# Row loads, an output slot and operand sums moved at the seam between two stages of a fused attention and gMLP kernel

## The chip, the cores and the metric

The kernel runs on one core of a Trainium2 chip. Its time is the device time of one execution in microseconds (us); eight runs of the kernel before gave a median of 776.43, from 775.05 to 778.31. The core has a matrix engine (TensorE, PE in the profile), a vector engine (VectorE, DVE), an activation engine (ScalarE, ACT), a general engine (GpSimd, POOL) and an engine that here only issues transfers (SyncE, SP). Each engine works through its own list of instructions in order and waits on semaphores for the others.

## The reference

The kernel computes a residual attention block and a residual gated MLP over 2048 tokens of width 1024. The part around the change is the MLP's gating, `_B_ref`:

```python
z = gelu(einsum('bsd,df->bsf', x, w_in))
z1 = z[..., :Fh]                       # Fh = 1792
z2 = layernorm(z[..., Fh:])
g = einsum('ts,bsf->btf', w_sp, z2) + b_sp[None, :, None]
return einsum('bsf,fd->bsd', z1 * g, w_out)
```

`w_sp` is 2048 x 2048 and `b_sp` has one value for each output token t.

## The kernel before

The kernel is one straight program. Every operation is recorded in program order, a recorder works out from the memory cells that each one reads and writes which others it has to wait for, and then each engine's list is emitted. There is no planner at run time: the order of the Python calls is the order of each engine's queue, transfers included (those of `sp` stand in SP's queue, those of `act` in ACT's).

The stages are attention with its output projection, then `z2` (the second half of the MLP's input, normalized and kept in fp16), then `z1` (the first half), then gating with the spatial matrix in two passes of 1024 output tokens each (`pr` 0 and 1), each followed by the product with `w_out`.

Both z1 and gating replace eight block products of a 2 x 2 block matrix product by seven, in a Strassen-like scheme, so both need sums of operands.

**z1.** `z1_step(g, k)` for 14 groups g and seven products k each (four matmuls per product). The steps run in the order of 7g + `offs[k]`; the last five are (13, 2) at 95 after (13, 7) at 94, then (12, 3) at 96, (13, 4) at 97 and (13, 3) at 103. Steps 6, 7, 4 and 3 are followed by adds on DVE into one of the `ZT` tiles, and `z1_out` on ACT writes the gelu into `Z1T`. The sums of weight blocks (`sz_sum`) run on POOL. With `on(g, k, f, ...)` other work is hung behind a step: the transposing loads of the four blocks of `w_sp` (`sp_load`, on SP's queue, at steps (6, 3), (8, 3) and (10, 3)), and their scaling to fp16 (`sp_part`, on ACT, groups 8 to 12).

**Operands of gating.** `b11`, `b12`, `b22` and `b21` are the scaled blocks of `w_sp`, 128 x 4096 each. `sp_sum` forms `t1 = b12 - b11`, `t2 = b22 - t1`, `t3 = b22 - b12` (into the memory of `b12`) and `t4 = b21 - t2`, for the first pass in four pieces of 128 x 1024, with a chosen engine for each piece. `s_sum(k, g)` forms the four sums `SS[:, 0]` to `SS[:, 3]` of blocks of `z2` for group g, 128 x 1024 each, on DVE; the second reads the first and the fourth reads the second.

**A group of gating.** `gate_group(pr, g, ba, bd, nx)` for g from 0 to 6. A product (`prod`) is eight matmuls into one of eight PSUM banks. `ba` holds the first product, `Z2 x b11`, made one group earlier. ACT copies it, scaled, to `s1`. POOL adds a row of biases to it twice, giving `s1b2` and `s1b1`. DVE then reads the other products with `stt` (bank times a scale plus an operand) and multiplies the four results into `Z1T` with `out`. The tiles `s1`, `s1b1`, `s1b2`, `u2` and `u3` exist once, so a group's values wait for the readers of the group before. In the first pass, groups 0 and 1 get both their first products (`b11` and `b21`) before group 0 starts: `pre` makes four products right after z1.

**Bias rows.** `brow_load(pr)` loads two stretches of 512 values of `b_sp`, each repeated on all 128 partitions, into `BROW[0]` and `BROW[1]` (at 205 K and 206 K of each partition's memory), with two transfers on SP's queue. The fifth slot of the weight sums `SZ` (used by z1 for odd groups) lies at 206 K too. After the row loads the same queue issues the two loads of `w_out` (`WO0`).

The seam between the stages in program order is: last z1 step; `t1` and `t2` in four pieces each; `s_sum` 1 to 4 for group 0; `brow_load(0)`; the `WO0` loads; four products; `gate_group(0, 0)`.

Of the kernel before, what the change touches and what calls it, by code (L numbers as in the profile page):

```python
# [6 lines left out]
F16 = mybir.dt.float16  # L7
# [251 lines left out]
def bass_sequential_preLN__memory_aug_infini_attn__mixer_gmlp__prompt_kernel(  # L259
# [17 lines left out]
    pe, act, dve, pool, sp = R.pe, R.act, R.dve, R.pool, R.sp  # L277

    K = 1024
# [4 lines left out]
    def tens(name, shape, dt, off):  # L284
        sz = int(np.prod(shape[1:])) * mybir.dt.size(dt)
        assert off % 32 == 0 and off + sz <= ARENA, (name, off, sz)
        t = nc.alloc_sbuf_tensor_at(name, list(shape), dt, offset=abase + off)
        R.space[t[:].tensor.name] = ("sbuf", off)
        return t

    class Bump:
# [4 lines left out]
        def __call__(self, name, shape, dt):  # L296
# [73 lines left out]
          for k, o in ROLES + (("t1", 126), ("t2", 190), ("t3", 22), ("t4", 38))}  # L370
# [3 lines left out]
           4: Z1X[:, 8:12, 1536:2048]},  # L374
          {1: tens("ht1", [128, 4, L], F16, 190 * K), 2: tens("ht2", [128, 4, L], F16, 194 * K),
           3: tens("ht3", [128, 4, L], F16, 38 * K), 4: tens("ht4", [128, 4, L], F16, 198 * K)}]
    SZ = [tens("sz%d" % i, [128, 4, 128], F16, o * K) for i, o in enumerate((58, 59, 60, 61, 206))]
    ZT = [tens("zt%d" % i, [128, L], F32, o * K) for i, o in enumerate((4, 6, 8, 10, 202, 12))]
    b3 = Bump(dead, 4 * K)
    ZST = b3("zst", [128, NTC, 4, 6], F32)  # L380
# [15 lines left out]
    BROW = [tens("brow%d" % i, [128, L], BF16, (205 + i) * K) for i in range(2)]  # L396
# [7 lines left out]
    def bank(b):  # L404
        return PS[:, b, :]
# [7 lines left out]
    def next_bank():  # L413
        b = rot["banks"][rot["n"] % len(rot["banks"])]
        rot["n"] += 1
        return b
# [555 lines left out]
    def sz(g, k):  # L972
        return SZ[k - 1 + (k == 4 and g % 2)][:]

# [75 lines left out]
    def sp_sum(o, r=None, eng=dve):  # L1050
        a, b = SUMS[o]
        s = slice(0, 8) if r is None else slice(2 * r, 2 * r + 2)
        eng.tensor_tensor(BH[o][:, s, :], BH[a][:, s, :], BH[b][:, s, :], ALU.subtract)

    def a_blk(i, j, g):
        f = 896 * i + 128 * g
        return Z2H[:, 8 * j:8 * j + 8, f:f + 128]

    def s_sum(k, g):
        if k == 1:  # L1060
            dve.tensor_tensor(SS[:, 0], a_blk(1, 0, g), a_blk(1, 1, g), ALU.add)
        elif k == 2:
            dve.tensor_tensor(SS[:, 1], SS[:, 0], a_blk(0, 0, g), ALU.subtract)
        elif k == 3:
            dve.tensor_tensor(SS[:, 2], a_blk(0, 0, g), a_blk(1, 0, g), ALU.subtract)
        else:
            dve.tensor_tensor(SS[:, 3], a_blk(0, 1, g), SS[:, 1], ALU.subtract)

    def prod(b, a, w, first):
        for i in range(8):  # L1070
            pe.matmul(bank(b), a[:, i, :], BH[w][:, i, :], start=(first and i == 0), stop=(i == 7),
                      skip_group_check=True)

    def prod1(g):
        b = next_bank()
        prod(b, a_blk(0, 0, g), "b11", True)
        return b
# [6 lines left out]
    def gate_group(pr, g, ba, bd=None, nx=True):  # L1084
        t1, t2 = slice(1024 * pr, 1024 * pr + 512), slice(1024 * pr + 512, 1024 * pr + 1024)
        s1, s1b1, s1b2, u2, u3 = (TMP[k][:] for k in ("s1", "s1b1", "s1b2", "u2", "u3"))
        inv = INV[0][:]

        def stt(o, b, add):
            dve.scalar_tensor_tensor(o, bank(b), inv, add, ALU.mult, ALU.add)  # L1090

        def out(v, i, t):
            z = Z1T[:, g + 7 * i, t]
            dve.tensor_tensor(z, v, z, ALU.mult)

        act.activation(s1, bank(ba), ACTF.Copy, scale=inv)
        pool.tensor_tensor(s1b2, s1, BROW[1][:], ALU.add)
        pool.tensor_tensor(s1b1, s1, BROW[0][:], ALU.add)
        if pr == 0 and g == 0:
            for r in range(4):  # L1100
                sp_sum("t3", r, pool if r < 2 else dve)
        bb, bc = next_bank(), next_bank()
        prod(bb, SS[:, 1], "t2", True)
        prod(bc, SS[:, 0], "t1", True)
        stt(u2, bb, s1b2)
        if pr == 0 and g == 0:
            for r in range(4):
                sp_sum("t4", r, pool if r < 2 else dve)
        nb = prod1(g + 1) if bd is None and g < 6 and nx else None
        if g < 6:  # L1110
            s_sum(1, g + 1)
            s_sum(2, g + 1)
        prod(bb, SS[:, 2], "t3", False)
        if bd is None:
            prod(ba, a_blk(0, 1, g), "b21", False)
        elif nx:
            nb = prod1(g + 2)
        stt(u3, bb, s1b2)
        stt(u3, bc, u3)
        out(u3, 1, t2)  # L1120
        if g < 6:
            s_sum(3, g + 1)
        prod(bb, a_blk(1, 1, g), "t4", False)
        stt(s1, ba if bd is None else bd, BROW[0][:] if bd is None else s1b1)
        out(s1, 0, t1)
        prod(bc, SS[:, 3], "b22", False)
        stt(s1b1, bb, s1b1)
        out(s1b1, 1, t1)
        stt(u2, bc, u2)
        out(u2, 0, t2)  # L1130
        if g < 6:
            s_sum(4, g + 1)
        return nb
# [17 lines left out]
    def brow_load(pr):  # L1151
        for k in range(2):
            t = 1024 * pr + 512 * k
            sp.dma_start(BROW[k][:], B_b_sp[t:t + 512].partition_broadcast(128))
# [8 lines left out]
    def z1_step(g, k):  # L1163
        p, fc = divmod(g, 7)
        s1, u2, u3 = ZT[g % 2][:], ZT[2 + g % 3][:], ZT[5][:]
        ka = {1: wz_blk(0, 0, fc), 2: wz_blk(0, 1, fc), 3: sz(g, 4), 4: wz_blk(1, 1, fc), 5: sz(g, 1),
              6: sz(g, 2), 7: sz(g, 3)}[k]
        kb = {1: hb(0, 0, p), 2: hb(1, 0, p), 3: hb(1, 1, p), 4: HT[p][4], 5: HT[p][1], 6: HT[p][2], 7: HT[p][3]}[k]
        first = k in (1, 6, 5)
        r = {1: 0, 2: 0, 6: 1, 7: 1, 4: 1, 5: 2, 3: 2}[k]  # L1170
        if first:
            zb[g, r] = next_bank()
        b = bank(zb[g, r])
        for i in range(4):
            pe.matmul(b, ka[:, i, :], kb[:, i, :], start=(first and i == 0), stop=(i == 3), skip_group_check=True)
        if k == 1:
            act.activation(s1, b, ACTF.Copy)
        if k == 6:
            dve.tensor_tensor(u2, b, s1, ALU.add)
        if k == 5 and g < 13:  # L1180
            for x in (1, 2):
                sz_sum(g + 1, x)
        if k == 7:
            dve.tensor_tensor(u3, b, s1, ALU.add)
            dve.tensor_tensor(u3, bank(zb[g, 2]), u3, ALU.add)
            z1_out(fc + 7, 2 * p + 1, u3)
            if g < 13:
                sz_sum(g + 1, 3)
        if k == 2:
            z1_out(fc, 2 * p, b)  # L1190
            if g == 0:
                sz_sum(1, 4)
        if k == 4:
            dve.tensor_tensor(s1, b, s1, ALU.add)
            z1_out(fc + 7, 2 * p, s1)
        if k == 3:
            dve.tensor_tensor(u2, b, u2, ALU.add)
            z1_out(fc, 2 * p + 1, u2)
            if g < 12:
                sz_sum(g + 2, 4)  # L1200
        for f, a in todo1.get((g, k), ()):
            f(*a)

    def on(g, k, f, *a):
        todo1.setdefault((g, k), []).append((f, a))
# [10 lines left out]
    for n, (k, g) in enumerate((("b11", 8), ("b12", 9), ("b22", 10), ("b21", 12))):  # L1216
        for r in range(4):
            on(g, (6, 7, 2, 4)[r], sp_part, k, r)
    offs = {1: -5, 6: 0, 5: 1, 7: 3, 2: 4, 4: 6, 3: 12}
    for x, g, k in sorted((7 * g + offs[k], g, k) for g in range(14) for k in offs):  # L1220
        z1_step(g, k)
    for k in ("t1", "t2"):
        for r in range(4):
            sp_sum(k, r)
    for k in range(1, 5):
        s_sum(k, 0)
    brow_load(0)
    for i in range(2):
        sp.dma_start(WO0[i][:], wout[:, 7 * i:7 * i + 7, 0:512])

    units = [(tc, 0, 512) for tc in range(6)] + [(tc, 512, 512) for tc in range(8)] + [(tc, 0, 512) for tc in (6, 7)]
    pre = [(prod1(g), prod2(g)) for g in range(2)]
    nb2 = gate_group(0, 0, *pre[0])
    nb = gate_group(0, 1, *pre[1])
    gate_group(0, 2, nb2, nx=False)
    for g in range(3, 7):
        nb = gate_group(0, g, nb)
# [73 lines left out]
```

## Time and profile before

| | |
|---|---|
| median of eight runs | 776.43 us (775.05 to 778.31) |
| profiled execution | 776.08 us, span of its instructions 774.3 us |
| busy PE / DVE / ACT / POOL | 753.2 / 552.0 / 373.7 / 293.1 us |
| z1's last matmuls, then the four products of `pre` | until 491.8, then 491.78 to 498.85 us |
| first pass of gating (first `t2` product to last `b22` product) | 504.50 to 589.5 us |
| second pass of gating | 637.65 to 723.5 us |

All times in the traces are microseconds from the start of the span, of one profiled execution. A line of a timeline gives the start, the duration, the engine, the operation with output and inputs by the program's names, the shape, and how many instructions are merged; in brackets stands the idle time of the engine before it and what ended that. `zt` are the z1 adds' tiles, `t1h` to `t4h` the fp16 sums of `w_sp` blocks, `ss` the sums of `z2` blocks, `tmp_s`, `tmp_s1b` and `tmp_u` are `s1`, (`s1b1`, `s1b2`) and (`u2`, `u3`). The chain of waits is followed back from the last instruction: each piece of it is work that the end waited for. Every operation is recorded through one helper, so all have the same line number and are told apart by tile.

### The profile page before, as it was taken

To read this page: it belongs to the slowest core of one execution; us is meant where nothing else is said; L and a number is where in the kernel's file an instruction comes from. 1 tells how busy PE (TensorE), PEld (TensorE's weight loads), DVE (VectorE), ACT (ScalarE), POOL (GpSimd) and SP (SyncE) were. 2 spreads that over 40 slices of the span, in tenths; PEclk is the share of its full clock that TensorE was granted. 3 is DMA by queue.
4 is the path that set the end of the run, shared out by engine and by line. 5 is a ranking of instruction groups with operands and counts; after the bars stand their busy time and mean duration, and the time that the engine had idled before them with its cause. 6 is when DMAs were issued, how large, how long until landed. Compare 5 with 4: busy or idle time off the path is not lost.

```text
span 774.3 us, 13304 instructions
## 1 busy us (share of the span) xinstructions
PE 753.2 (97%) x5422; PEld 361.2 (47%) x5496; DVE 552.0 (71%) x956; ACT 373.7 (48%) x433; POOL 293.1 (38%) x430
## 2 busy tenths in 40 slices
PE   8999999999999999999999999789999999999998
PEld 3445555455555545455554444334444444444444
DVE  5586589768964676659867975899895566889422
ACT  6777876787777677156966799500000000000000
POOL 2564556555553333100089887441330002223000
PEclk9999999999999999999999999989999999999999
DMA  9554555353425332797510074300038950000122
GB/s 300 169 153 89 97 83 124 82 97 84 97 55 130 90 82 42 198 248 226 182 58 1 1 133 92 102 1 1 0 55 145 242 191 8 1 0 1 62 82 75
DMA packets 138078, 75.08 MB, mean 97 GB/s; under 512 B 98336, under 2 KB 128800, under 8 KB 138016
## 3 DMA queue, kind: packets, MB, share of 16 engines
q1 hardware_dynamic: 130768, 67.40, 36.0%
q10 hardware_dynamic: 7248, 6.82, 3.0%
q8 instruction: 43, 0.70, 0.4%
q14 instruction: 19, 0.16, 0.1%
HBM read 42.74 MB, written 8.39 MB: 66 GB/s over the span
## 4 chain that ended last, share of the span: by engine, by line
PE 77%; DVE 11%; ACT 4%; DMA 3%; issue 3%; POOL 2%; ACTq 0%; POOLq 0%; DVEq 0%
PE ps L210 77%; ACT sj L210 3%; DVE ss L210 2%; DMA sj<-in_B_w_sp_dram 2%; DVE tmp_u L210 2%; DVE z1T L210 1%; ACT z L210 1%; POOL sz L210 1%; POOL zrs L210 1%; DMA wv<-in_A_wv_dram 1%; DVE stats L210 1%; DVE zt L210 1%; DVE t2h L210 1%; DVE tmp_s L210 0%; DVE tmp_s1b L210 0%
## 5 line engine op out<-in xcount | busy, mean ns | idle before, releaser
L210 ACT ACTIVATE e<-ps 128x2048 bf16<-128x2048 f32 (+1 forms) x96 | 152.6, 1590 | 41.7 <-PE ps L210 41.4
L210 POOL TENSOR_SCALAR_AFFINE_SELECT e<-e 128x512 bf16<-128x512 bf16 x128 | 90.8, 722 | 132.0 <-ACT e L210 131.9
L210 ACT ACTIVATE tmp_s<-ps,inv 128x512 f32<-128x512 f32 x14 | 9.6, 688 | 208.8 <-DVE z1T L210 146.9
L210 POOL TENSOR_TENSOR tmp_s1b<-tmp_s,brow 128x512 f32<-128x512 f32 x28 | 43.0, 1555 | 175.9 <-ACT tmp_s L210 165.9
L210 PE MATMUL ps<-win,hnT 128*128 128x448 bf16 x512 | 98.4, 352 | 0.0
L210 PE MATMUL ps<-w_out,z1T 128*128 128x512 bf16 x328 | 73.2, 379 | 0.4
L210 PEld LDWEIGHTS ps<-win,hnT 128*128 128x128 bf16 x512 | 49.6, 98 | 46.3 <-issue 0.2
L210 DVE TENSOR_TENSOR fin<-fin,ps 128x512 bf16<-128x512 bf16 (+2 forms) x33 | 21.9, 670 | 56.8 <-PE ps L210 41.0
L210 DVE TENSOR_TENSOR zt<-ps,zt 128x512 f32<-128x512 f32 x70 | 47.7, 688 | 20.6 <-PE ps L210 17.2
L210 PE MATMUL ps<-xnT,wk 128*128 128x512 bf16 x233 | 59.6, 380 | 1.2
L210 PE MATMUL ps<-wv,xnT 128*128 128x512 bf16 x255 | 59.5, 380 | 1.2 <-DMA wv<-in_A_wv_dram 0.8
L210 PE MATMUL ps<-wo,oT 128*128 128x512 bf16 x254 | 57.7, 380 | 0.1
L210 PE MATMUL ps<-xnT,wq 128*128 128x512 bf16 x226 | 54.0, 379 | 1.6
L210 PEld LDWEIGHTS ps<-w_out,z1T 128*128 128x128 bf16 x336 | 32.9, 98 | 39.7
L210 ACT ACTIVATE z<-ps 128x448 bf16<-128x448 f32 x60 | 30.6, 550 | 34.9 <-PE ps L210 34.9
L210 PEld LDWEIGHTS ps<-v,e 128*128 128x128 bf16 x1280 | 38.8, 96 | 14.0 <-issue 6.5
L210 DVE BATCH_NORM_STATS2 zst<-z 128x6 f32<-128x448 bf16 x64 | 37.8, 608 | 8.6 <-ACT z L210 8.5
L210 PE MATMUL ps<-v,e 128*128 128x33 bf16 x1280 | 42.2, 178 | 0.0
L210 DVE RECIPROCAL rd<-ps 128x16 f32<-128x16 f32 x32 | 8.0, 250 | 47.0 <-PE ps L210 46.8
L210 PEld LDWEIGHTS ps<-wo,oT 128*128 128x128 bf16 x256 | 24.1, 98 | 27.5
L210 PEld LDWEIGHTS ps<-xnT,wk 128*128 128x128 bf16 x256 | 22.6, 98 | 29.9 <-issue 5.0
L210 PEld LDWEIGHTS ps<-wv,xnT 128*128 128x128 bf16 x256 | 23.1, 98 | 28.1 <-DMA wv<-in_A_wv_dram 1.5
(168 smaller groups left out, 1381.0 us busy)
## 6 DMA issues: line engine op xcount, KB each, us to landing
sj<-in_B_w_sp_dram SPq DMA_DIRECT2D x16, 512.0 KB, 3.5
xch<-in_A_x_dram SPq DMA_DIRECT2D x16, 256.0 KB, 3.6
xr<-in_A_x_dram SPq DMA_DIRECT2D x16, 256.0 KB, 4.1
out_dram<-hch SPq DMA_DIRECT2D x16, 256.0 KB, 2.4
win<-in_B_w_in_dram SPq DMA_DIRECT2D x4, 896.0 KB, 5.3
wz<-in_B_w_in_dram SPq DMA_DIRECT2D x6, 512.0 KB, 7.4
wo<-in_A_wo_dram SPq DMA_DIRECT2D x1, 2048.0 KB, 8.4
fin<-out_dram ACTq DMA_DIRECT2D x16, 128.0 KB, 3.4
```

The costliest lines, as they stand in the source:

```text
L210: ins = getattr(e, op.name)(*op.args, **op.kw)
```

## The change

Five edits are made. The fifth `SZ` slot moves from 206 K to 204 K. `brow_load(0)` is issued behind z1 step (7, 3) instead of after z1. The four pieces of `t1` are formed behind z1 step (12, 3), so ahead of steps (13, 4) and (13, 3). `s_sum` 3 and 4 of group 0 move from the end of z1 into group 0, ahead of the `t3` and ahead of the `t4` pieces; and of the `t3` pieces POOL forms one (the first) instead of two, DVE three. In every group of both passes the first output is formed in `u3` instead of `s1`.

```diff
-    SZ = [... for i, o in enumerate((58, 59, 60, 61, 206))]
+    SZ = [... for i, o in enumerate((58, 59, 60, 61, 204))]
...
         pool.tensor_tensor(s1b1, s1, BROW[0][:], ALU.add)
         if pr == 0 and g == 0:
+            s_sum(3, 0)
             for r in range(4):
-                sp_sum("t3", r, pool if r < 2 else dve)
+                sp_sum("t3", r, dve if r else pool)
         bb, bc = next_bank(), next_bank()
         prod(bb, SS[:, 1], "t2", True)
         prod(bc, SS[:, 0], "t1", True)
         stt(u2, bb, s1b2)
         if pr == 0 and g == 0:
+            s_sum(4, 0)
             for r in range(4):
                 sp_sum("t4", r, pool if r < 2 else dve)
...
-        stt(s1, ba if bd is None else bd, BROW[0][:] if bd is None else s1b1)
-        out(s1, 0, t1)
+        stt(u3, ba if bd is None else bd, BROW[0][:] if bd is None else s1b1)
+        out(u3, 0, t1)
...
+    for r in range(4):
+        on(12, 3, sp_sum, "t1", r)
+    on(7, 3, brow_load, 0)
+
     offs = {1: -5, 6: 0, 5: 1, 7: 3, 2: 4, 4: 6, 3: 12}
     for x, g, k in sorted((7 * g + offs[k], g, k) for g in range(14) for k in offs):
         z1_step(g, k)
-    for k in ("t1", "t2"):
-        for r in range(4):
-            sp_sum(k, r)
-    for k in range(1, 5):
-        s_sum(k, 0)
-    brow_load(0)
+    for r in range(4):
+        sp_sum("t2", r)
+    s_sum(1, 0)
+    s_sum(2, 0)
```

More of the change, by code (lines that the diff above doesn't have):

```diff
@@ L376, in bass_sequential_preLN__memory_aug_infini_attn__mixer_gmlp__prompt_kernel @@
            3: tens("ht3", [128, 4, L], F16, 38 * K), 4: tens("ht4", [128, 4, L], F16, 198 * K)}]
-    SZ = [tens("sz%d" % i, [128, 4, 128], F16, o * K) for i, o in enumerate((58, 59, 60, 61, 206))]
+    SZ = [tens("sz%d" % i, [128, 4, 128], F16, o * K) for i, o in enumerate((58, 59, 60, 61, 204))]
     ZT = [tens("zt%d" % i, [128, L], F32, o * K) for i, o in enumerate((4, 6, 8, 10, 202, 12))]
```

## The prediction

> **What bounds the kernel now.** The page's first part has TensorE (PE) busy 97% of the span, so a change can pay only where PE stands still. The page's row of slices dips to 7 and 8 in one place alone, 484 to 523 us, where the clock's row dips too: the seam where z1 ends and gating begins. Next I read the chain that ended last there:
>
> ```profile
> 491.98 0.69 DVE zt L210
> 492.67 2.40 DVE t1h L210 x4
> 495.07 4.33 DVE t2h L210 x4
> 499.40 2.53 DVE ss L210
> ...
> 501.96 6.20 DVE ss L210 x3
> ...
> 509.42 1.28 DVE t3h L210 x2
> ```
>
> From the last z1 add at 491.98 to the first read of group 0's second product (`stt(u2, bb, s1b2)`, called U here) at 510.62, the path is VectorE (DVE) alone. The four `t1` pieces cost 0.60 each, yet four `ss` sums of the same 128x1024 f16 size cost 2.5. The timelines of GpSimd (POOL), DVE and PE say why:
>
> ```profile
> 496.14 2.71 POOL L210 TENSOR_TENSOR tmp_s1b<-tmp_s,brow 128x512 f32<-128x512 f32 x2 [9.96 <-DMA brow<-in_B_b_sp_dram]
> 498.82 5.08 POOL L210 TENSOR_TENSOR t3h<-b22h,b12h 128x1024 f16<-128x1024 f16 x2
> ```
>
> ```profile
> 499.33 2.60 DVE L210 TENSOR_TENSOR ss<-z2h 128x1024 f16<-128x1024 f16 x1
> ...
> 523.15 0.67 DVE L210 TENSOR_TENSOR ss<-z2h 128x1024 f16<-128x1024 f16 x1
> ```
>
> ```profile
> 504.50 3.60 PE L210 MATMUL ps<-t2h,ss 128*128 128x512 f16 x8 [5.65 <-DVE ss L210]
> ```
>
> While POOL runs a sum, each DVE sum ends about 0.5 us after the POOL instruction in progress (499.33 to 501.93, POOL's first `t3` ending near 501.38), and POOL's next one then starts late. The two alternate: one POOL sum (two of `t3`, then two of `t4`) and one DVE sum take 2.52 together (10.09 for four, 499.33 to 509.42), where the DVE sum alone takes 0.60. So a POOL sum under a busy DVE costs the path 1.92. The wait for `brow` looks large (9.96) but ended at 496.14; its share is judged below.
>
> After the seam DVE stays the path through groups 0 and 1, and again between groups 5 and 6 of either pass, where PE has six products instead of seven. In the other groups it is PE: the read `stt(u3, bb, s1b2)` (called A) waits 1.33 for PE. One crossing, from A of group 5 to U of group 6:
>
> ```profile
> 577.96 3.17 POOL L210 TENSOR_TENSOR tmp_s1b<-tmp_s,brow 128x512 f32<-128x512 f32 x2 [8.92 <-ACT tmp_s L210]
> ```
>
> ```profile
> 572.91 0.75 DVE L210 SCALAR_TENSOR_TENSOR tmp_u<-ps,inv,tmp_s1b 128x512 f32<-128x512 f32 x1 [1.33 <-PE ps L210]
> ...
> 579.24 0.87 DVE L210 TENSOR_TENSOR z1T<-tmp_u,z1T 128x512 bf16<-128x512 f32 x1
> 580.03 1.64 DVE L210 TENSOR_TENSOR ss<-z2h,ss 128x1024 f16<-128x1024 f16 x1
> 581.59 0.74 DVE L210 SCALAR_TENSOR_TENSOR tmp_u<-ps,inv,tmp_s1b 128x512 f32<-128x512 f32 x1
> ```
>
> PE had then waited 0.89 for U. A to U takes 8.68. Without POOL the two caught instructions would start 0.61 apart and U would start at 580.45: the two POOL adds cost 1.14 per crossing.
>
> **The seam, part by part.** (1) `t1` moves ahead of the last two z1 adds. They are DVE instructions at 491.12 and 491.98; the add before them starts at 490.25, so `t1` starts at 490.86 instead of 492.59: 1.73 gained, and the two adds then follow at 0.61 each: 1.22 back. Net 0.51. Behind the four pieces queue those two adds (the second now ends near 494.6), ACT's two gelus of them and ACT's `s1`, now at about 495.2 to 495.9 instead of 493.71. PE does not notice: the two banks that the late adds read are taken again only by later products, after its 7.1 us of four ready ones (491.78 to 498.85).
>
> (2) The row load costs SP two issues (0.33 to 0.58 each), ahead of the `b22` transposes. They were issued until 466.00, land after 4.1 in the median, and ACT reads them at 473.11: 3.0 of slack cover 1.05. It also brings little: POOL's first add could start at 496.14 before and now waits for `s1`, to about 496. The load hides a wait that (1) would bring anyway. At nothing.
>
> (3) One `t3` piece goes from POOL to DVE: five POOL instructions instead of six before the path is free. That takes away 1.92 and adds one DVE sum of 0.60: net 1.32. (4) `s_sum(4,0)` goes behind U: it stays on DVE, so U comes 0.6 earlier still, the sums behind it do not. `b22`'s product, which reads it, is three products behind.
>
> Sum: U at 510.62 - 0.51 - 1.32 - 0.60 = 508.2, so PE starts the `t3` product near 509.0 instead of 511.42; A of group 0, which stands behind U and behind the moved sum either way, gains 0.51 + 1.32 and goes from 513.81 to 512.0: **1.83**. The product of `t2` starts when the second `ss` is done, near 502.0 instead of 504.50; even at the halved clock of before (3.60 for eight matmuls) it ends by 505.6, before U.
>
> **The crossings.** The first output now goes to `u3`, so DVE no longer reads `s1`, and ACT's next `s1` is ready long before. POOL's first add of the next group then waits only for A, which reads the old `s1b2`; the second only for the product of `s1b1` with z1T. On the times of the crossing shown: A ends at 573.66, the add starts at 573.73 (ACT to POOL took 0.07) and takes 1.13 undisturbed (the pair at 640.35 took 2.27), to 574.86. The z1T product asks at 574.48, is held until 574.86 and frees DVE 0.49 later instead of 0.61 after its start: 0.26 lost. The `s1b1` product then ends at 578.81; the second add runs 578.88 to 580.01. The instruction between reads PSUM, and such ones were not held (0.74 beside POOL); the next z1T product asks at 579.50: 0.39 lost. Together 0.65 instead of 1.14, so **0.49** per crossing, with no third instruction caught. Both ends of this unseen order: nothing lost at all (1.14 gained), or both products held for a whole add (2.26, so 1.12 lost). I take the 0.49, as the instants of asking stand in rows.
>
> Four crossings are on the path (0 to 1, 1 to 2, and 5 to 6 in both passes): 1.96. PE allows it: it stood still 1.33, 0.89, 0.89 and 0.89 there. In all other crossings DVE had 1.33 to spare, so they gain nothing. Sum 1.83 + 1.96 = 3.8. The profiled execution took 776.08 (span 774.3, 1.8 around it), 0.35 under the median of 776.43. So 776.08 becomes 772.3, and the median **772.6**.
>
> **The clock, which could take some back.** PE's longest new gap is before `t3` of group 1: six products from 509.0 at 1.73 each, and 0.16 for the last to end, reach 519.5; U there (A at 512.0 + 8.19) ends near 520.9: 1.45 instead of 1.33. The stretches of 3.41, with PE's busy time (and matmuls), then granted clock, DMA share and GB/s:
>
> ```profile
> 498.97:502.38 3.41, 0.00 (x0) 1.00 0.39 125
> 502.38:505.79 3.41, 1.29 (x4) 0.50 0.02 5
> 505.79:509.21 3.42, 3.42 (x10) 0.50 0.00 0
> ...
> 519.44:522.86 3.42, 2.51 (x12) 1.00 0.01 2
> ```
>
> A stretch with no matmul was followed by 6.83 at half clock; one with 2.51 of 3.42 busy was not. A gap of 1.45 leaves 1.96, between the two and nearer to 2.51, so I take no drop; a drop would cost 1.7 (one stretch) to 3.4 (two). [...]
>
> **Rivals.**
> R1, the crossings bring nothing or half: 1.83 to 2.8 gained, 773.6 to 774.6. For it: every add at a crossing is recorded with 1.60, not 1.13, and no row shows the new order. Against: in those records POOL starts while a DVE product of two SBUF operands is still running, so the 0.47 is waiting. 0.17.
> R2, the clock drops after a gap: 774.3 to 776.0. For and against as above. 0.08.
> R3, slower: the adds, released in the middle of DVE's chain, hold two DVE instructions each crossing for 0.95 (the 1.64 against 0.69 seen) to 1.13 (a whole add). Its place is the z1T product after A and that after `s1b1`. 1.90 to 2.26 instead of 1.14, four times, is 3.0 to 4.5, less the seam's 1.83: 777.6 to 779.1. It decides from 1.60 lost per crossing. Against: A and the product's asking are 0.82 apart, and an add ends 0.38 after that; it would have to be released 0.6 later than any release seen. 0.10.
> R4, the row loads hold the transposes: if each waited for a landing (3.2 to 4.3), ACT, busy 36.81 of 37.00 us before the seam, would get `b22` 1.8 to 5.6 late: 774.4 to 778.2. Against: in attention loads and transposes alternate on this queue and land in 2.9 and 3.7. 0.05.
> The forecast keeps 0.60, with its own spread of 0.7 (POOL's phase, a self-wait of 0.1 per sum).
>
> **Numbers.** About 0.2%, 1.55 us, can be told from no change. Faster: 0.60 + 0.17 + half of R2 = 0.81. Slower: most of R3, 0.08. Within: 0.11. The range reaches up to 775.1, over R1 and half of R2; R3, nearly all of R4 and the other half, 0.18, are left out. Down it goes to 771.4: if the crossings lost nothing, they would bring 0.65 more once and 0.40 three times (up to PE's 0.89), 1.85 in all, of which I take in 1.2.
>
> **What would show it.** Right: `t1` from 490.9 on; three DVE `ss`, not four, between `t2` and U, at about 1.6, 2.5 and 2.5, then a `t3` piece at 2.5 and two at 0.6; U near 508.2 and A at 512.0; POOL's adds apart, one behind A and one behind the `s1b1` product; A to U 8.2; PE's gap before group 6 about 0.4. Wrong: an `ss` or z1T product above 1.2 at a crossing (R3), a clock below 1.00 after 512 (R2), ACT idle near 473 (R4), or A to U still 8.7 (R1).

## The result and the profile after

The changed kernel takes 773.43 us (median of 13 runs, 772.5 to 774.94) against 776.11 (median of 35 runs of the kernel before): a ratio of 0.9964 [0.9956, 0.9973], so 2.8 us less (2.1 to 3.4). The forecast was 3.8. The profiled execution took 773.94 us, its span 772.2. That span is only 2.1 below the 774.3 of before because z1 happened to end 0.97 later in it; over all profiles shown here z1's end lies anywhere from 491.3 to 495.1. (Two waits of PE before 413 us make it later here, 1.11 and 0.56. u3_only below, which has none of the edits to z1, has both, 0.83 and 0.56; pe_fill, which has all of them, has neither.) So instants are compared below as distances from z1's end (the start of the first `pre` product: 491.78 before, 492.75 after).

The chain of waits of the changed kernel, across the seam:

```profile
491.91 2.40 DVE t1h L210 x4
494.31 1.20 DVE zt L210 x2
495.51 2.40 DVE t2h L210 x4
497.92 0.61 DVE ss L210
498.53 0.02 issue
498.55 3.09 DVE ss L210 x2
501.64 0.46 DVE t3h L210
502.10 1.99 issue
504.09 5.12 DVE t3h L210 x2
509.21 0.67 DVE tmp_u L210
```

The edits are all there: `t1` ahead of the two last `zt` adds, three `ss` sums, then three `t3` pieces, then U at 509.13. POOL's timeline shows the first `t3` piece between the adds and `t4`, and the two adds of a later crossing standing apart:

```profile
496.93 4.16 POOL L210 TENSOR_TENSOR tmp_s1b<-tmp_s,brow 128x512 f32<-128x512 f32 x2 [9.78 <-ACT tmp_s L210]
501.06 2.56 POOL L210 TENSOR_TENSOR t3h<-b22h,b12h 128x1024 f16<-128x1024 f16 x1
503.58 5.08 POOL L210 TENSOR_TENSOR t4h<-b21h,t2h 128x1024 f16<-128x1024 f16 x2
...
572.55 1.16 POOL L210 TENSOR_TENSOR tmp_s1b<-tmp_s,brow 128x512 f32<-128x512 f32 x1 [5.77 <-DVE tmp_u L210]
577.72 1.16 POOL L210 TENSOR_TENSOR tmp_s1b<-tmp_s,brow 128x512 f32<-128x512 f32 x1 [4.00 <-DVE z1T L210]
```

DVE's timeline, at the seam and at the crossing from group 5 to 6:

```profile
495.43 2.48 DVE L210 TENSOR_TENSOR t2h<-b22h,t1h 128x1024 f16<-128x1024 f16 x4
497.84 0.68 DVE L210 TENSOR_TENSOR ss<-z2h 128x1024 f16<-128x1024 f16 x1
498.55 1.53 DVE L210 TENSOR_TENSOR ss<-ss,z2h 128x1024 f16<-128x1024 f16 x1
500.01 1.64 DVE L210 TENSOR_TENSOR ss<-z2h 128x1024 f16<-128x1024 f16 x1
501.57 7.64 DVE L210 TENSOR_TENSOR t3h<-b22h,b12h 128x1024 f16<-128x1024 f16 x3
...
513.56 0.75 DVE L210 SCALAR_TENSOR_TENSOR tmp_u<-ps,inv,tmp_s1b 128x512 f32<-128x512 f32 x1 [0.56 <-PE ps L210]
...
573.29 0.97 DVE L210 TENSOR_TENSOR z1T<-tmp_u,z1T 128x512 bf16<-128x512 f32 x1
...
578.33 1.09 DVE L210 TENSOR_TENSOR z1T<-tmp_u,z1T 128x512 bf16<-128x512 f32 x1
579.35 0.68 DVE L210 TENSOR_TENSOR ss<-z2h,ss 128x1024 f16<-128x1024 f16 x1
```

Before, one `z1T` took 0.87 and the `ss` behind it 1.64 at this crossing; now the two `z1T` take 0.97 and 1.09 and the `ss` its bare 0.68. The bracket at 513.56 is new: A of group 0 waits 0.56 for PE. PE's timeline says why, and the windows of 3.41 us of PE alone (PE's busy time with matmuls, granted clock, DMA share, GB/s) show it in the clock:

```profile
500.14 1.90 PE L210 MATMUL ps<-t2h,ss 128*128 128x512 f16 x8 [0.32 <-DVE ss L210]
501.88 1.89 PE L210 MATMUL ps<-t1h,ss 128*128 128x512 f16 x8
509.93 3.60 PE L210 MATMUL ps<-t3h,ss 128*128 128x512 f16 x8 [6.16 <-DVE tmp_u L210]
513.32 2.50 PE L210 MATMUL ps<-b11h,z2h 128*128 128x512 f16 x8
...
580.74 1.90 PE L210 MATMUL ps<-t3h,ss 128*128 128x512 f16 x8 [0.42 <-DVE tmp_u L210]
```

```profile
502.38:505.79 3.41, 1.39 (x7) 1.00 0.02 5
505.79:509.21 3.42, 0.00 (x0) 0.78 0.00 0
509.21:512.62 3.41, 2.69 (x7) 0.50 0.00 0
512.62:516.03 3.41, 3.41 (x13) 0.72 0.00 0
```

Before, PE's one long gap (5.65) stood ahead of the `t2` product, and that product had slack. Now the gap of 6.16 stands ahead of `t3`, whose result A reads: 3.60 for eight matmuls instead of 1.90.

Where the time went, each instant from z1's end:

| | before | after | earlier by | forecast |
|---|---|---|---|---|
| U of group 0 | 18.84 | 16.38 | 2.46 | 2.43 |
| A of group 0 | 22.03 | 20.81 | 1.22 | 1.83 |
| `t3` product of group 1 | 31.50 | 29.82 | 1.68 | 2.32 |
| `t3` product of group 2 | 42.93 | 40.77 | 2.16 | 2.81 |
| `t3` product of group 6 | 90.61 | 87.99 | 2.62 | 3.30 |
| from there to the `t3` product of group 6 in pass 2 | 134.02 | 133.54 | 0.48 more | 0.49 more |

The sum, 2.62 and 0.48, is 3.1, a little above the timed 2.8 and inside its interval. The four crossings bring 0.46 to 0.48 each; the seam, which was to give A the 1.83, gives it 1.22, 0.61 less than forecast, though U came as forecast.

### The profile page after: what moved, and what is told of

Read it like the earlier page. It is cut to its first block, busy times and chain, and to the rows that moved or that the text cites. A ratio compares the mean times of both kernels' runs of the same rounds, so it can differ in the third digit from the quotient of the medians.

```text
span 772.2 us, 13342 instructions
## 1 busy us (share of the span) xinstructions
PE 753.7 (98%) x5422; PEld 361.4 (47%) x5496; DVE 545.1 (71%) x957; ACT 373.5 (48%) x433; POOL 281.8 (36%) x429
## 4 chain that ended last, share of the span: by engine, by line
PE 79%; DVE 9%; ACT 4%; issue 3%; DMA 3%; POOL 2%; POOLq 0%; ACTq 0%; DVEq 0%
PE ps L210 79%; ACT sj L210 3%; DMA sj<-in_B_w_sp_dram 2%; DVE tmp_u L210 1%; POOL sz L210 1%; POOL zrs L210 1%; ACT z L210 1%; DVE ss L210 1%; DVE zt L210 1%; DVE t3h L210 1%; DVE stats L210 1%; DVE z1T L210 1%; DMA xch<-in_A_x_dram 0%; DVE hch L210 0%; DVE t2h L210 0%
## 5 line engine op out<-in xcount | busy, mean ns | idle before, releaser
L210 POOL TENSOR_TENSOR tmp_s1b<-tmp_s,brow 128x512 f32<-128x512 f32 x28 | 34.2, 1224 | 183.5 <-ACT tmp_s L210 69.6
L210 DVE BATCH_NORM_STATS2 zst<-z 128x6 f32<-128x448 bf16 x64 | 37.7, 608 | 10.6 <-ACT z L210 10.4
L210 DVE SCALAR_TENSOR_TENSOR tmp_u<-ps,inv,tmp_s1b 128x512 f32<-128x512 f32 x30 | 22.3, 744 | 25.0 <-PE ps L210 22.0
L210 DVE TENSOR_TENSOR z1T<-tmp_u,z1T 128x512 bf16<-128x512 f32 x42 | 37.0, 882 | 1.4
```

What stands on the lines that cost most here:

```text
L210: ins = getattr(e, op.name)(*op.args, **op.kw)
```

## The experiments

The measured 2.8 is 1.0 short of the forecast. Theory 1 says that the crossings bring what was forecast and that the part missing is the clock's, lost at the seam behind PE's gap. Theory 2 gives the seam its full 1.83 and the crossings about 1.0 in all. Both share one reading of the seam, called the lock reading below: DVE sums and POOL sums of SBUF operands alternate (2.52 for one of each in the kernel before), and a POOL sum costs the path 1.92.

### One half of the change each

**u3_only** (before, with the first output formed in `u3`):

```diff
-        stt(s1, ba if bd is None else bd, ...)
-        out(s1, 0, t1)
+        stt(u3, ba if bd is None else bd, ...)
+        out(u3, 0, t1)
```

> The kernel before with the one edit that the first output is formed in u3. The measured gain of the whole change, 2.8, is 1.0 short of the 3.8 forecast. Theory 1 (clock): the crossings bring what was forecast, 4 x 0.49 = 1.96, and the seam brings too little because PE's idle time came in one piece of 6.16 us and the t3 product behind it ran at half clock (3.60 instead of 1.90). Then this kernel stays 1.9 to 2.0 below the kernel before (ratio 0.9975), A to U takes 8.2. Theory 2 (crossings): the seam brought its 1.83 and the four crossings only 1.0 together; then this kernel is 1.0 below (0.9987) or less.

Measured: 774.66 us, 0.9972 [0.9960, 0.9985]. The profile shows PE's gaps of 0.42 before groups 2 and 6, so the crossings gain here as they do in the whole change. That much answers theory 2. The time itself says less, because the seam moved too, though no edit touches it: U came at 16.92 instead of 18.84. POOL's first add was recorded at 498.06, not at the same place among the `t2` pieces, and `t2`'s four pieces ran undisturbed in 2.49. A (21.37) kept 0.66 of the 1.92. PE had a gap of 6.17 and `t3` ran at half clock (3.59), but A doesn't wait for PE here: DVE's timeline has no idle time before it, and the two `t4` pieces behind U, held by POOL's, take 2.54, where before they took 1.28. That is the 1.26 that A lost.

```profile
510.73 2.54 DVE L210 TENSOR_TENSOR t4h<-b21h,t2h 128x1024 f16<-128x1024 f16 x2
...
514.51 0.74 DVE L210 SCALAR_TENSOR_TENSOR tmp_u<-ps,inv,tmp_s1b 128x512 f32<-128x512 f32 x1
```

**seam_only** (after, with the first output in `s1` again):

```diff
-        stt(u3, ba if bd is None else bd, ...)
-        out(u3, 0, t1)
+        stt(s1, ba if bd is None else bd, ...)
+        out(s1, 0, t1)
```

> The changed kernel with the first output formed in s1 again; all that is left is the seam. Theory 1 (clock): U early by 2.4 against z1's end as forecast, but the t3 product at half clock puts A at 1.2 early instead of 1.83, so 1.2 below the kernel before (0.9985). Theory 2 (crossings): 1.8 below (0.9976), and the half clock is paid from idle time.

Measured: 775.65 us, 0.9990 [0.9980, 1.0001]. Theory 2's 0.9976 lies just outside; by the time alone the edits of the seam can't be told from no change. In the profile A comes 1.38 earlier than before (20.65), nearer to theory 1's 1.2 than to theory 2's 1.8. The seam is as in the whole change, the slow product with it (3.42), and the gaps of 0.89 and 0.90 before groups 1 and 2 are back. PE's timeline of seam_only:

```profile
511.22 3.42 PE L210 MATMUL ps<-t3h,ss 128*128 128x512 f16 x8 [6.17 <-DVE tmp_u L210]
...
524.17 1.90 PE L210 MATMUL ps<-t3h,ss 128*128 128x512 f16 x8 [0.89 <-DVE tmp_u L210]
535.59 1.90 PE L210 MATMUL ps<-t3h,ss 128*128 128x512 f16 x8 [0.90 <-DVE tmp_u L210]
```

The halves bring 2.2 and 0.8 by the ratios; they can't simply be added, since the seam of u3_only moved too.

### Work in PE's gap

**pe_fill** (after; group 2's first product, which is ready, is made during group 0's gap, and three times over, only to keep PE busy; it does 16 matmuls more than after):

```diff
+        if bd is not None and nx and g == 0:
+            nb = next_bank()
+            for _ in range(3):
+                prod(nb, a_blk(0, 0, g + 2), "b11", True)
         prod(bb, SS[:, 2], "t3", False)
...
-        elif nx:
+        elif nx and g:
             nb = prod1(g + 2)
```

> The changed kernel with PE's gap before group 0's t3 product filled: the first product of group 2, which nothing holds back, is made there three times over (24 matmuls, 5.2 us; the last one counts) instead of once behind t3. Theory 1: the clock stays full, t3 takes 1.90, A comes 0.64 earlier and the kernel is 0.65 below the changed one, 3.4 below the kernel before (0.9956). Theory 2: no change against the changed kernel (2.8 below, 0.9964).

Measured: 772.38 us, 0.9951 [0.9933, 0.9968]. PE's timeline:

```profile
502.36 5.34 PE L210 MATMUL ps<-b11h,z2h 128*128 128x512 f16 x24
508.70 1.90 PE L210 MATMUL ps<-t3h,ss 128*128 128x512 f16 x8 [1.00 <-DVE tmp_u L210]
```

U stands where after has it (16.40), yet `t3` takes 1.90 and A comes at 20.19: 1.84 earlier than before, against 1.83 in the forecast's sum. From z1's end to group 6 it gains 3.25, with pass 2's crossing 3.72. The mean granted clock is 1.000 in all six executions of pe_fill and 0.996 or less in all of after. Time alone doesn't tell it from theory 2's number; the profile does. Theory 1 holds: the 0.61 is the clock's (A at 20.81 in after, 20.19 here).

### The price of a POOL sum

**all_dve** (after; DVE forms every `t3` and `t4` piece) and **before_all_dve** (the kernel before with the same two lines):

```diff
-                sp_sum("t3", r, dve if r else pool)
+                sp_sum("t3", r, dve)
...
-                sp_sum("t4", r, pool if r < 2 else dve)
+                sp_sum("t4", r, dve)
```

> The changed kernel with all eight t3 and t4 pieces on DVE, none on POOL. If a POOL sum under a busy DVE costs the path 1.92 and a DVE piece 0.60 (the lock reading, theories 1 and 2 alike), U comes 5.2 earlier (three POOL sums less, one DVE piece more), A 4.0 to 4.6 earlier, PE's long gap falls to 1.0 with the clock full, and the kernel is 4.0 to 4.6 below the changed one: 6.8 to 7.4 below the kernel before (0.991). A gap of 2.7 then stands before group 1's t3 product; if the clock falls there, 1.7 to 3.4 less. Rival (the DVE sums are slow for another reason, memory or operands): the three more DVE pieces make it 1.8 slower than the changed kernel.

> The kernel before with the t3 and t4 pieces all on DVE and nothing else. If a POOL sum under a busy DVE costs 1.92 and a DVE piece 0.60, A comes 4 x (1.92 - 0.60) = 5.3 earlier, at 16.7 after z1's end, and the kernel is 5.3 below the kernel before (0.9932). What is left of the change on top of it (head start 0.5, four crossings 0.49 each) would then be the 2.4 between this and all_dve (0.9896). If the change's gain and POOL's are the same gain, this one comes out like all_dve.

Measured: 768.67 us, 0.9896 [0.9880, 0.9913], and 770.85 us, 0.9930 [0.9915, 0.9945]. DVE's timeline of all_dve:

```profile
499.32 1.64 DVE L210 TENSOR_TENSOR ss<-z2h 128x1024 f16<-128x1024 f16 x1
500.88 2.48 DVE L210 TENSOR_TENSOR t3h<-b22h,b12h 128x1024 f16<-128x1024 f16 x4
503.29 0.74 DVE L210 SCALAR_TENSOR_TENSOR tmp_u<-ps,inv,tmp_s1b 128x512 f32<-128x512 f32 x1
```

Four `t3` pieces now take 2.48, where three took 7.64. U comes 5.15 earlier than in after (11.23 from z1's end) although DVE forms one piece more ahead of it. PE's longest gap is 1.37 (the gap of 2.7 that was expected before group 1's `t3` product is 1.13), and the clock is 1.000 in every execution of both kernels. In before_all_dve A comes 5.16 earlier (16.87), where 5.3 was expected. Two lines on the kernel before bring 5.4 us by the ratio (4.3 to 6.6), more than the whole change: the engine "relieved" by POOL was the one that paid. The lock reading holds, and so does its price. The rival, that these sums are slow for a reason of their own, had all_dve 1.8 slower than after; it is out.

**t3_two_pool** (after, with two `t3` pieces on POOL again):

```diff
-                sp_sum("t3", r, dve if r else pool)
+                sp_sum("t3", r, dve if r > 1 else pool)
```

> The changed kernel with two of the four t3 pieces on POOL, as before, and two on DVE. By the lock reading DVE's chain up to A gets 1.92 - 0.60 = 1.3 longer, part of it behind U; since A waited 0.56 for the t3 product at half clock in the changed kernel, 0.6 to 0.8 of it is left: 0.6 to 0.8 above the changed kernel (ratio to the kernel before 0.9973), A relative to z1's last product 0.6 later. Were the piece's place indifferent, no change (0.9964).

Measured: 774.07 us, 0.9970 [0.9957, 0.9983]; its time can't be told from after's, nor from the 0.6 to 0.8 above it that was expected. U comes at 13.87, earlier than after's 16.38, since fewer POOL sums were done before it; but one now stood behind U and held the moved `s_sum` (1.94 instead of 0.68) and a `t4` piece. A came at 20.85 against 20.81, without a wait for PE. DVE's timeline behind U:

```profile
507.42 1.94 DVE L210 TENSOR_TENSOR ss<-z2h,ss 128x1024 f16<-128x1024 f16 x1
509.29 3.21 DVE L210 TENSOR_TENSOR t4h<-b21h,t2h 128x1024 f16<-128x1024 f16 x2
```

PE's timeline shows the idle time in two pieces:

```profile
507.55 1.90 PE L210 MATMUL ps<-t3h,ss 128*128 128x512 f16 x8 [3.65 <-DVE tmp_u L210]
...
514.54 1.90 PE L210 MATMUL ps<-t4h,z2h 128*128 128x512 f16 x8 [3.36 <-DVE tmp_u L210]
```

In this execution the clock stayed full; in the other six the mean granted clock was 0.996 or 0.998. So the `t3` edit, which the forecast put at 1.32, brought nothing at A: in after the clock took 0.6, and at full clock (pe_fill, A at 20.19) it is worth 0.66: of the two POOL sums that reach behind U here, one held DVE for only 1.26 (1.94 less 0.68) instead of 1.92.

### The head start of `t1` and the row load

**t1_late** (after; `t1` behind z1 again):

```diff
-    for r in range(4):
-        on(12, 3, sp_sum, "t1", r)
...
+    for k in ("t1", "t2"):
+        for r in range(4):
+            sp_sum(k, r)
-    for r in range(4):
-        sp_sum("t2", r)
```

> The changed kernel with the t1 pieces behind both last z1 adds again, all else as changed. Forecast of the prediction: 0.5 of head start lost (1.73 less 1.22), so U and t3's product 0.5 later, the kernel 0.5 above the changed one (0.997). Rival: the whole 1.73 counts (0.9986), or nothing, since POOL's adds come earlier by the same amount (0.9964).

Measured: 774.7 us, 0.9982 [0.9971, 0.9993], slower than expected. Both late z1 adds now stand ahead of `t1`, so ACT's `s1` comes sooner, POOL starts at 494.02 (2.70 after z1's end; 4.18 in after), and its adds and sums catch every `t2` piece. DVE's and PE's timelines:

```profile
494.54 8.25 DVE L210 TENSOR_TENSOR t2h<-b22h,t1h 128x1024 f16<-128x1024 f16 x4
...
509.80 0.75 DVE L210 SCALAR_TENSOR_TENSOR tmp_u<-ps,inv,tmp_s1b 128x512 f32<-128x512 f32 x1 [1.37 <-PE ps L210]
```

```profile
506.09 3.59 PE L210 MATMUL ps<-t2h,ss 128*128 128x512 f16 x8 [7.69 <-DVE ss L210]
```

The `t2` product comes late, after a gap of 7.69 and at half clock, and U waits 1.37 for it. So the value of the head start by itself isn't measured here: the edit also moves POOL against DVE.

**brow_late** (after; the row load behind z1 again, with the `SZ` slot put back):

```diff
-    SZ = [... (58, 59, 60, 61, 204))]
+    SZ = [... (58, 59, 60, 61, 206))]
...
-    on(7, 3, brow_load, 0)
...
     s_sum(2, 0)
+    brow_load(0)
```

> The changed kernel with the row loads after z1 and the fifth SZ slot at 206 K again. Forecast: worth nothing, since s1 comes at about the time when the rows landed (4.3 after z1's last matmul): same as the changed kernel within 0.3 (0.9964). Rival: the wait of 9.96 for brow was worth something, then 1 or more above the changed kernel (0.998).

Measured: 773.06 us, 0.9963 [0.9950, 0.9976]; the early row load brings nothing that can be told. POOL's first add waited for the row until 499.42 and caught a `t2` piece. PE's timeline:

```profile
505.35 2.99 PE L210 MATMUL ps<-t2h,ss 128*128 128x512 f16 x8 [3.20 <-DVE ss L210]
...
512.27 1.90 PE L210 MATMUL ps<-t3h,ss 128*128 128x512 f16 x8 [1.60 <-DVE tmp_u L210]
```

The clock fell here too, but on the `t2` product, for which U doesn't wait; `t3` took 1.90, and A came at 20.18, as in pe_fill. So by this profile the place of the gap decides what it costs. The times can't show the 0.63: brow_late's and after's can't be told apart, and the profiled execution was the slowest of the eight (775.68).

**all_dve_t1early** and **all_dve_t1mid** (all_dve, with `t1` placed earlier still):

```diff
-        on(12, 3, sp_sum, "t1", r)
+        on(12 + r // 2, (4, 6)[r // 2], sp_sum, "t1", r)   # t1early
+        on(13, (6, 7)[r // 2], sp_sum, "t1", r)            # t1mid
```

> The changed kernel with all t3 and t4 pieces on DVE and t1 in pairs behind z1 steps (12, 4) and (13, 6), where DVE stood idle 1.1 before the adds of step (13, 7). If DVE's chain is still the path, t2 starts 1.0 to 1.5 earlier and the kernel is that much below all_dve: 8.5 to 9.5 below the kernel before (0.988). If the late adds now hold PE's banks or ACT, no gain on all_dve (0.9896) or a loss.

> As all_dve, with t1 in pairs behind z1 steps (13, 6) and (13, 7). With the pairs behind (12, 4) and (13, 6), t3's product of group 1 came 1.9 earlier against z1's end, but PE waited 0.86 inside z1 for the late add of step (13, 6). Here that add is ahead of t1: no PE wait in z1, t2 about 1.0 earlier than in all_dve, so 1.0 below all_dve (ratio to before 0.988). If the late adds hold PE all the same, no gain.

Measured: 768.19 us, 0.9898 [0.9883, 0.9913], and 767.42 us, 0.9881 [0.9863, 0.9900]. The first brings `t3` of group 6 1.89 nearer to z1's end than all_dve, but z1 itself waits, and the time can't be told from all_dve's. PE's timeline of all_dve_t1early:

```profile
488.75 1.04 PE L210 MATMUL ps<-ht,sz 128*128 128x512 f16 x4 [0.86 <-DVE zt L210]
```

The second puts two pieces into each of two places where DVE had waited for PE in all_dve (1.13 and 0.31), as DVE's timeline of all_dve_t1mid shows, and PE doesn't wait in z1:

```profile
487.80 1.28 DVE L210 TENSOR_TENSOR t1h<-b12h,b11h 128x1024 f16<-128x1024 f16 x2
489.01 1.42 DVE L210 TENSOR_TENSOR zt<-ps,zt 128x512 f32<-128x512 f32 x2
490.34 1.28 DVE L210 TENSOR_TENSOR t1h<-b12h,b11h 128x1024 f16<-128x1024 f16 x2
```

It is the fastest median, by its ratio 9.2 us below before (7.8 to 10.6). Over all_dve it is 1.49 better from z1's end in the profile; the intervals of the two times overlap.

### The same kernels once more

**before_again**, **after_again** (unchanged, profiled a second time):

> The kernel before, profiled once more. Reading: at the seam DVE and POOL take turns, and which DVE instruction POOL's first add catches depends on when the bias rows land. If so, the sums' total up to A stays (A 21.4 to 22.3 after z1's end, 22.0 in the first profile), while the start of the t2 product and PE's long gap may lie elsewhere (12.72 and 5.65 in the first profile; 7.92 and 6.17 in the kernel with u3 alone, whose seam has the same instructions). If the seam is the same in each execution, both stay.

> The changed kernel, profiled once more. Here the first add waits for s1 and not for a transfer, so the seam should come out as in the first profile: t2 product 7.4 after z1's end, gap of 6.16, t3 product at half clock (3.4 to 3.6), A at 20.8. A clock that falls at another instant can bring A to 20.2 to 21.4.

Measured, single runs: 775.6 and 773.52 us. From z1's end, before's U lies at 18.84 in both profiles, after's at 16.38 and 16.39; the slow `t3` product is there again (3.60 after 6.17). In these two pairs the meeting of POOL and DVE repeats within 0.03 us; u3_only was profiled once, so whether its other meeting is its program's or that execution's stays open.

## Why the prediction was right, and where it was off

**Lock and U: right.** From z1's end U came 2.46 earlier against 2.43 forecast. The price of a POOL sum also holds outside the forecast (before_all_dve: 5.16 at A, 5.3 expected). Beside POOL's adds of the crossing (572.55 and 577.72 in the changed kernel) the `z1T` products, both of whose operands lie in SBUF, are held, 0.97 and 1.09 instead of 0.69; the reads of PSUM are not, 0.74 and 0.75. Who is held can't be told from the recorded starts: see the last section.

**The way to U: not as told.** I expected the sums at 1.6, 2.5 and 2.5, then one `t3` piece at 2.5 and two at 0.6. The profile has 0.68, 1.53 and 1.64, then three pieces in 7.64. POOL's sums stood later against DVE's, so the collisions fell on `t3` pieces rather than on `ss` sums. The number of them before U was the same, and so was the sum.

**The split of the 1.83: not as told.** At full clock A is 1.84 earlier (pe_fill), as the sum had it. But t3_two_pool, which has every edit except that of the `t3` pieces, is already 1.18 earlier at A (22.03 to 20.85), where the forecast's other terms give 0.51; and the `t3` edit brings 0.66 on top (20.85 to 20.19), where it was put at 1.32. The 0.67 that the former bring too much is about what u3_only gained at A (0.66) with no edit at the seam; in both profiles one POOL sum that lies partly beside U costs 1.26 instead of 1.92. That the two misses cancel is luck.

**The failed step: A, and the clock.** The forecast has "The product of `t2` starts when the second `ss` is done, near 502.0 instead of 504.50", and from that "PE's longest new gap is before `t3` of group 1". The second `ss` ended at 500.1 already (499.1 with z1's end as before), because the first `ss` met no POOL sum and the second only an add, and the `t2` product started at 500.14. PE was through with all that it had by 503.8 and idled 6.16 until `t3`. The forecast had followed PE at this place only so far as to see that `t2` ended before U; how long PE would then stand was not worked out. Its own instants already had a longer gap than 1.45 there: two products from 502.0, at 1.73 and 1.89, end near 505.6, and `t3` was put near 509.0, which leaves 3.4 (an estimate from these numbers). R2 had the mechanism ("the clock drops after a gap"), but at another place and at 1.7 to 3.4; its sign, a clock below 1.00 after 512, did appear (0.72 from 512.62 to 516.03). Measured, it cost 0.61 at A: of the one slow product that A reads, 1.70 longer than at full clock, most fell into slack, and A waited 0.56 for it. pe_fill gives it back.

**The crossings: right.** A to U of the first one went from 8.68 to 8.22 (513.56 to 521.78), a gain of 0.46 against 0.49; all four bring 1.88 against 1.96. PE's gap before group 6 is 0.42, as forecast. R1 and R3 are out: an add lasts 1.16 with nothing in its way, and no `z1T` or `ss` of the crossing shown takes longer than 1.09.

**The row load: right at nothing** (brow_late), though the load did change which instruction POOL caught. R4 did not occur: ACT reads `b22` from 474.1 on, without any idle time before those reads.

**The clock behind short and long gaps.** The short gaps around the seam (0.32 to 1.37 in all_dve, 0.33 to 1.89 in pe_fill) left the clock at 1.000 in every execution of these two kernels. Gaps of 5.65, 6.16, 6.17 and 7.69 were followed by half clock in every profile that has one: the eight matmuls behind took 3.42 to 3.60 instead of 1.90. Between them the profiles show no sharp bound: the clock fell behind the gap of 3.20 in brow_late and stayed full behind those of 3.65 and 3.36 in t3_two_pool. One execution of each of these two kernels kept a mean of 1.000, and the others did not.

## What to carry to other kernels

Price work given to a helper engine by what it blocks, not by the helper's idle time: here a POOL sum of 128x1024 cost the path 1.92, while DVE forms it itself in 0.60. Follow TensorE's idle time even where TensorE is off the path: several short waits (up to 1.37 in all_dve) left the clock full here, yet gathered into one gap of 6.16 they halved the clock of the product behind (3.60 instead of 1.90 in the changed kernel). Filling the gap with ready products prevented it (1.90 in pe_fill, which makes one product three times over; whether once is enough was not tried). And when work is moved ahead into an earlier stage, put it where that engine already waits: `t1` cost z1 0.86 in one place and nothing a step later.

## What had not been expected of the hardware

The order in which POOL and DVE get through here isn't that of their starts in the records. POOL's first add is recorded at 496.93 in the changed kernel, 0.30 ahead of the last of four back-to-back `t2` pieces (497.23), and yet that piece and the first `ss` ran undisturbed (2.48 for the four pieces, 0.68), and the add held only the second `ss` (1.53). In the kernel before the add is recorded 0.06 ahead of the third piece and did get in (4.41 for the four pieces). Which of DVE's instructions an add catches could not be worked out from the profile of before, and the runs leave it open. In u3_only POOL's start lay 0.56 later from z1's end than before (4.92 against 4.36), with no edit at the seam, and U came 1.92 earlier, A 0.66. A forecast of such a place has at least this spread, even though both kernels that were profiled twice repeated themselves.
